# Retention followed by a Mish layer: one copy on another engine, one tile's columns reordered, two PSUM banks exchanged

## The chip, the cores and the metric

The kernel runs on one core of a Trainium2 chip. TensorE (PE) multiplies and writes to PSUM, eight banks of 128 x 512 float32; VectorE (DVE) and ScalarE (ACT) copy and compute out of PSUM; GpSimd (POOL) works between tiles in SBUF and issues most loads; SyncE (SP) issues stores. The metric is the device time of one execution in microseconds, the median of several runs. Beside it one execution was recorded with the profiler; times of single instructions come from that one.

## What is computed

Retention over 8 batches, 8 heads, 576 positions and 64 dimensions, and behind it a layer with Mish on the 4608 rows:

```python
scores = scale * np.matmul(q, k.transpose(0, 1, 3, 2))
Dmat = np.where(rel >= 0, gamma[:, None, None] ** rel[None, :, :], 0.0)     # rel = i - j, one gamma per head
attn = np.matmul(scores * Dmat[None], v)
x = attn.transpose(0, 2, 1, 3).reshape(B * S, H * D)       # 4608 x 512
h = x @ w_in                                               # 4608 x 2048
out = (h * np.tanh(softplus(h))) @ w_out                   # 4608 x 512, float32
```

## The kernel before

The 4608 rows are cut into chunks of 128 rows of one batch, 36 in all (the last 64 rows of two batches share one), and four chunks make a tile of 512 rows; there are nine tiles. Tiles 0 and 1 hold the first chunk of every batch, four batches each. The other chunks follow in pairs. `N0` is 8, the first chunk behind the two first tiles.

A tile goes through three stages. First its `xT` is made: x transposed, bf16, 128 partitions by 4 blocks of 128 features (`KC`) by 512 rows. Then `gT` = Mish(x w_in): for each of 16 blocks of `w_in`, TensorE adds four products into an `hp` bank and ScalarE applies Mish (`g1`, lines 587 and 603). Then g times `w_out`, done with seven half-size block products instead of eight: `unit(t, k)` issues half of product i of tile t (`seven`, line 672), and `taken` moves the result out of its bank or adds it to others. The sums that these products need are made by VectorE from `gT` and `w_out` (`g_sum`, line 663; `w_sum`, line 653).

The first chunks need no past: `f_scores`, `f_out` and `f_v` compute them directly. `f_out(1, b, (act, dve))` makes x of tile 1 for two batches in a double bank `sc`, and copies each batch's half to `xT` (line 262), ScalarE the first and VectorE the second. Tile 1 is then multiplied with `w_in` in two halves, two batches each: `g1_half(i, j)` issues eight products of 256 rows for two blocks of `w_in` (line 612) and one Mish of 512 columns (line 614). `x1[j]` is the view of `xT` for half j.

Each batch also carries a state, k transposed times v summed over chunks. `first_states(t, j)` computes the first states of the four batches of tile t into two banks, `st` and `ops` (line 300), half of the rows with j = 0 and the rest with j = 1; `first_states_copy(t, copies)` copies the banks to SBUF with the two engines that it is given (line 311). For tile 1 that is called within the second half of `g1_half`, before its blocks 6 and 7.

From there on chunks come in pairs in a `visit(n, banks, copies)`: the states of the next pair (`states`, line 448), the outputs of this pair into two banks (`outputs`, line 504, and `outputs_end`, line 520), the scores of the next pair (`step_s`, line 402), then the two banks copied to `xT` by ScalarE (line 532), and the scores masked by VectorE (`step_m`, line 408). Each chunk before its visit is scaled by VectorE (`step_p`, line 359, for q and k; `step_v`, line 366, for v) and its q and k are transposed by TensorE (`step_t`, line 382) and copied by ScalarE (lines 385, 386 and 388). `states` leaves a list of sums that VectorE adds up (line 472) and a cast for ScalarE (lines 479 and 482).

The order on every engine is written out by hand: an engine takes its instructions in the order in which the code issues them, and waits are put in where tiles and banks depend on each other. Between the two first tiles and the steady loop stands a list of steps u = 2 to 23, which runs the products of tile 0 (`unit(0, u - 2)`), then those of tile 1 (`unit(1, u - 16)`), the first two visits (u = 16 and u = 22) and the loads of coming chunks. Loads run through GpSimd's queue (line 342); each waits for the chunk two before it to land and for a free buffer.

PSUM is divided into four pools: `sc` has two double banks, `hp` two banks, `st` and `ops` one bank each. A new tile in a pool waits until the one that had the bank before has been read. In `unit` a table, `beside`, names the products that take another pool than `ops`. For tile 1 the products come in the order 4, 3, 2, 1, 6, 5, 7; 4 takes `hp`, 3 takes `st`, 2 and 1 take `ops`, and 6 and 7 are added to the banks of 3 and 5. The second visit (u = 22) stands between the products i = 2 and i = 1 of that tile. `taken` copies product 2 out of its bank with ScalarE (line 697), and product 1 as well (line 703).

Of the kernel before, what the change touches and what calls it, by code (L numbers as in the profile page):

```python
# [16 lines left out]
def kernel(  # L17
# [18 lines left out]
    nc = tc.nc  # L36
    B, H, S, D = q.shape
    assert (B, H, S, D) == (8, 8, 576, 64)
    P = 128
# [4 lines left out]
    KC = d_model // P  # L44
# [15 lines left out]
    N0 = 2 * NCH  # L60
# [12 lines left out]
    ps_st = ctx.enter_context(tc.tile_pool(name="ps_st", bufs=1, space=PS))  # L73
    ps_h = ctx.enter_context(tc.tile_pool(name="ps_h", bufs=2, space=PS))
    ps_o = ctx.enter_context(tc.tile_pool(name="ps_o", bufs=1, space=PS))
# [4 lines left out]
    w_in_t = wpool.tile([P, KC, d_ff], BF16)  # L80
# [19 lines left out]
    fst = {}  # L100
# [133 lines left out]
    x1 = []  # L234

    def f_out(t, b, copy):
        if b == 0:
            xts[t] = xp.tile([P, KC, NCH * P], BF16, name="xT")
            if t == 1:
                x1.extend(xts[1].rearrange("p c k -> p (c k)")  # L240
                          .rearrange("p (j c k) -> p j c k", j=2, c=KC)[:, j] for j in range(2))
        vb = fst[t]["vb"][b]
        if t == 0:
            pool, name = ((ps_h, "hp"), (ps_h, "hp"), (ps_st, "st"), (ps_o, "ops"))[b]
            ot = pool.tile([P, NP, P], F32, name=name)
        else:
            if b % 2 == 0:
                fst[1]["out"] = ps_sc.tile([P, 2, NP, P], F32, name="sc")
            ot = fst[1]["out"][:, b % 2]
        for p in range(NP):  # L250
            for e in range(2):
                nc.tensor.matmul(ot[ds(64 * e, 64), p, :], lhsT=vb[:, 2 * p + e, :],
                                 rhs=fst[t]["sm", b][:, 2 * p + e, :],
                                 start=(p == 0), stop=True, skip_group_check=True)
        if t == 0:

            n = NP if b < 2 else NP // 2
            for p in range(0, NP, n):
                copy(xts[t][:, ds(p, n), ts(b, P)], ot[:, ds(p, n), :])
        elif b % 2:  # L260
            for e in range(2):
                copy[e](x1[b // 2][:, :, ts(e, P)], fst[1]["out"][:, e])  # L262

    def f_state(t, b, engine=nc.gpsimd):

# [42 lines left out]
    def first_states_copy(t, copies):  # L308
        for i in range(2):
            pair = first.tile([P, 2, NP, 64], F32, name="s0", bufs=4)  # L310
            copies[i](pair, s0_banks[t][i])
            for x in range(2):
                s0[4 * t + 2 * i + x] = pair[:, x]
# [117 lines left out]
    def written(products):  # L431
        sync = mybir.DependencyInfo(mybir.DependencyClass.Sync, mybir.DependencyReason.DATA)
        seen = nc.sync.nop()
        for ins in products:
            tc.add_manual_dep(seen.ins, ins.ins.name, sync, reason="row halves and a bank")
        return seen
# [53 lines left out]
    def run(jobs, *how):  # L490
        while jobs:
            jobs.pop()(*how)
# [4 lines left out]
    def outputs(n, both):  # L497

        for x in range(2):
            vs = live[n + x]["vs"]  # L500
            for h in range(NP):
                for j in range(2):
                    for a in range(2):
                        nc.tensor.matmul(both[j][ds(64 * a, 64), h, x, :], lhsT=vs[ds(64 * j, 64), 2 * h + a, :],
                                         rhs=live[n]["sm"][ds(64 * j, 64), h % 2, x, 2 * (h // 2) + a, :],
                                         start=(x == 0 and h == 0), stop=False, skip_group_check=True)

    def outputs_end(n, both, other, seen=None):

        made = []  # L510
        for x in range(2):
            b, c = chunks[n + x]
            qk = live[n + x]["qk"]
            for g in range(2):
                for e in range(2):
                    j = e ^ other
                    state = st_sb[b, c, j] if c < 4 else st_sb[b + j, 4]
                    for a in range(2):
                        r, p = ds(64 * e, 64), 2 * g + a
                        made.append(nc.tensor.matmul(  # L520
                            both[j][ds(64 * a, 64), 2 * g + e, x, :], lhsT=state[r, p, :],
                            rhs=qk[r, 0, p, ds(64 * j, 64)], start=False, stop=True, skip_group_check=True))
                        if seen is not None and len(made) == 1:
                            behind(made[0], seen)
        return made[-4:]
# [8 lines left out]
    def visit(n, banks, copies, masked=True):  # L534


        units = states(n + 2)
        for unit in units[:1]:
            unit()
        both = [pool.tile([P, NP, 2, 64], F32, name=name) for pool, name in banks]  # L540
        outputs(n, both)
        seen = written(outputs_end(n, both, 0))
        if units:
            step_s(n + 2)
        for unit in units[1:]:
            unit()
        outputs_end(n, both, 1, seen)
        outputs_copy(n, both, copies)
        if units and masked:
            step_m(n + 2)  # L550
# [54 lines left out]
    def g1_half(i, j):  # L605

        if 1 not in gts:
            gts[1] = gp.tile([P, nF, NCH * P], BF16, name="gT")
        hp = ps_h.tile([P, 2, 2 * P], F32, name="hp")
        for a in range(2):  # L610
            for c in range(KC):
                nc.tensor.matmul(hp[:, a], lhsT=w_in_t[:, c, ts(2 * i + a, P)], rhs=x1[j][:, c, :],  # L612
                                 start=(a == 0 and c == 0), stop=(c == KC - 1), skip_group_check=True)
        nc.scalar.activation(gts[1][:, ds(2 * i, 2), ds(2 * P * j, 2 * P)], hp, AX.Mish)  # L614

# [19 lines left out]
    NS = 2  # L635
# [40 lines left out]
    dve, act, pool = nc.vector.tensor_copy, nc.scalar.copy, nc.gpsimd.tensor_copy  # L676
# [78 lines left out]
    def unit(t, k):  # L755

        i, half = ORDER.get(t, (4, 2, 1, 3, 6, 5, 7))[k // 2], k % 2
        if half == 0 and i not in LIKE:
            beside = {5: (ps_st, "st"), 4: (ps_h, "hp"), 3: (ps_h, "hp")} if t == 0 else \
                {4: (ps_h, "hp"), 3: (ps_st, "st")} if t < NS else \  # L760
                {2: (ps_st, "st"), 3: (ps_st, "st")} if t == nT - 2 else {}
            pool, name = beside.get(i, (ps_o, "ops"))
            banks[i] = pool.tile([P, 2, hD], F32, name=name)
        bank = banks[LIKE.get(i, i)]
        seven(t, i, half, bank, add=i in LIKE)
        if half:
            taken(t, i, bank)
# [252 lines left out]
    for i in range(8):  # L1020
        if i == 1:
            ahead(7)
            load(N0 + 3)
            g_sum(0, 2)
            for m in (7, 4):
                w_sum(m)
        elif i == 4:
            first_states(1, 0)
        elif i == 6:
            first_states(1, 1)  # L1030
            first_states_copy(1, (act, dve))
        g1_half(i, 1)

    queued = [4 * NCH]
# [13 lines left out]
    for u in range(2, 24):  # L1048
        j, w = divmod(u, 4)
        for m in {2: (6,), 3: (3, 1)}.get(u, ()):  # L1050
            w_sum(m)
        if u in (5, 7):
            g_sum(0, 1 if u == 5 else 6)
        if u in ps:
            att(N0 + ps[u], "P")
        if u == 11:
            step_m(N0)
        if u in vs:
            att(N0 + vs[u], "V")
        if u in (19, 21):  # L1060
            g_sum(1, 1 if u == 19 else 6)
        for s in {14: (0, 1), 17: (2, 3)}.get(u, ()):
            send(0, s)
        if w == 0 and j > 0:
            if j < 5:
                load(N0 + j + 3)
            else:
                more_loads(N0 + j + PF)
        if u == 10:
            units = states(N0)  # L1070
            units[0]()
            step_s(N0)
            units[1]()
            run(sums)
        elif u == 16:
            visit(N0, ((ps_o, "ops"), (ps_st, "st")), (act, act), masked=False)
            g_sum(1, 2)
            run(sums)
            att(N0 + 5, "P")
            att(N0 + 4, "V")  # L1080
            step_m(N0 + 2)
        elif u == 22:
            visit(N0 + 2, ((ps_h, "hp"), (ps_h, "hp")), (act, act))
        if u in (13, 20):
            run(casts, act)
        if u in ts_:
            att(N0 + ts_[u], "T")
        if u < nF:
            if u == 15:
                att(N0 + 4, "P")  # L1090
            unit(0, u - 2)
            flush()
        else:
            unit(1, u - nF)
# [136 lines left out]
```

## Time and profile before

| what | before |
|---|---|
| median of 3 runs | 291.44 us (291.42 to 293.78) |
| profiled execution, its time | 292.62 us |
| its span | 290.9 us |
| TensorE busy | 276.6 us, 95% |
| VectorE busy | 220.5 us, 76% |
| ScalarE busy | 160.6 us, 55% |
| GpSimd busy | 154.5 us, 53% |
| granted TensorE clock | 0.998 |
| moved by DMA | 45.95 MB |

The span is what the profiler records between the first and the last instruction; the time of the execution has some 1.7 us around it. A share of busy time is a mean over the whole span, in which stages with different limits follow each other. In a row of the timeline stand the start, the time taken, the engine, the line, the operation, the tile written and the tiles read, the shape, and in brackets the idle time of the engine before it with what ended it. A row of waits has who waited, for whom, and then the total, the number of times and the longest.

### The profile page before, as it was taken

What the parts mean: (1) busy time and instruction counts of PE and PEld (TensorE: products, weight loads), DVE (VectorE), ACT (ScalarE), POOL (GpSimd) and SP (SyncE); (2) the same over time, 40 slices, a digit from 0 to 9 for tenths busy, and PEclk for the clock granted to TensorE, in tenths of its full rate; (3) what the DMA queues carried; (4) which work ended last, traced back from release to release, by engine and by line L of the source; (5) the groups of instructions that cost most, each with busy time, mean ns of one, the idle gap of its engine ahead of it and who ended that gap; (6) DMA issues with size and microseconds to landing.
All of it is one profiled execution on the core that took longest, in us unless ns stands there. A gap on an engine that the chain in (4) does not pass through costs nothing.

```text
span 290.9 us, 9142 instructions
## 1 busy us (share of the span) xinstructions
PE 276.6 (95%) x3960; PEld 205.2 (71%) x3988; DVE 220.5 (76%) x312; ACT 160.6 (55%) x284; POOL 154.5 (53%) x183
## 2 busy tenths in 40 slices
PE   8699999996999989999999999999999999999994
PEld 8567688885877656666666666667666766888783
DVE  4873587899999885888389877883989194778783
ACT  5556566633766654645474646465646455476620
POOL 8487696756581986274818473938240000369500
PEclk9999999999999999999999999999999999999999
DMA  7999999789999597959996999599939001200333
GB/s 152 209 204 218 221 198 217 190 183 227 277 215 202 120 192 221 214 147 138 229 186 186 144 239 190 159 137 245 164 101 146 0 5 72 74 1 2 103 92 97
DMA packets 42600, 45.95 MB, mean 158 GB/s; under 512 B 23872, under 2 KB 32320, under 8 KB 42560
## 3 DMA queue, kind: packets, MB, share of 16 engines
q0 software_dynamic: 15312, 30.15, 50.4%
q1 hardware_dynamic: 26656, 14.69, 25.6%
q8 instruction: 31, 0.51, 0.8%
q10 hardware_dynamic: 592, 0.52, 0.6%
q14 instruction: 9, 0.07, 0.1%
HBM read 36.70 MB, written 9.44 MB: 159 GB/s over the span
## 4 chain that ended last, share of the span: by engine, by line
PE 80%; DVE 9%; issue 3%; DMA 3%; POOL 2%; ACT 1%; POOLq 0%; ACTq 0%; DVEq 0%
PE hp L587 29%; PE ops L672 26%; PE hp L612 4%; PE hp L592 3%; DMA gT<-in_v_dram 3%; PE st L672 2%; DVE qks L359 2%; PE hp L672 2%; PE hp L809 2%; PE sc L809 1%; PE sc L448 1%; DVE vs L366 1%; DVE room L663 1%; PE sc L880 1%; PE sc L402 1%
## 5 line engine op out<-in xcount | busy, mean ns | idle before, releaser
L587 PE MATMUL hp<-xT,w_in_t 128*128 128x512 bf16 x380 | 96.9, 379 | 1.4
L603 ACT ACTIVATE gT<-hp 128x512 bf16<-128x512 f32 x113 | 67.1, 598 | 45.8 <-PE hp L587 40.2
L672 PEld LDWEIGHTS <-room 128*128 128x128 bf16 x656 | 63.4, 98 | 14.6 <-DVE room L663 0.6
L587 PEld LDWEIGHTS <-w_in_t 128*128 128x128 bf16 x412 | 39.9, 98 | 35.3 <-issue 0.2
L359 DVE TENSOR_TENSOR qks<-qkraw,gqk 128x512 bf16<-128x512 f32 x56 | 46.9, 886 | 9.4 <-DMA qkraw<-in_k_dram 6.2
L663 DVE TENSOR_TENSOR room<-gT 128x2048 bf16<-128x2048 bf16 x43 | 52.7, 1245 | 1.1 <-ACT gT L603 1.1
L672 PE MATMUL ops<-room,room 128*128 128x256 bf16 x336 | 42.0, 273 | 0.5 <-DVE room L663 0.4
L366 POOL TENSOR_TENSOR vs<-vraw,gv 128x512 bf16<-128x512 f32 x20 | 26.0, 1319 | 22.6 <-ACT gT L603 22.5
L342 POOL DMA_DIRECT2D vraw<-in_v_dram x24 | 21.2, 887 | 25.9 <-issue 24.7
L672 PEld LDWEIGHTS <-gT 128*128 128x128 bf16 x288 | 27.5, 98 | 7.9 <-issue 1.7
L342 POOL DMA_DIRECT2D qkraw<-in_q_dram x24 | 21.6, 899 | 13.6 <-DVE vs L366 3.1
L408 DVE TENSOR_TENSOR sm<-sc,mask 128x1024 bf16<-128x1024 f32 x14 | 17.1, 1218 | 15.5 <-PE sc L402 14.0
L672 PE MATMUL ops<-w_out_t,room 128*128 128x256 bf16 x224 | 27.2, 273 | 0.0
L827 POOL TENSOR_TENSOR vraw<-vraw 128x256 f32<-128x256 f32 x7 | 6.4, 908 | 38.2 <-ACT vraw L821 38.1
L342 POOL DMA_DIRECT2D qkraw<-in_k_dram x24 | 21.3, 886 | 0.0
L612 PE MATMUL hp<-xT,w_in_t 128*128 128x256 bf16 x128 | 15.2, 273 | 0.4 <-DVE xT L262 0.4
L472 DVE TENSOR_TENSOR total<-sc,total 128x256 f32<-128x256 f32 x32 | 13.5, 422 | 2.2 <-PE sc L448 1.4
L672 PE MATMUL ops<-room,gT 128*128 128x256 bf16 x112 | 13.9, 272 | 1.3 <-issue 1.2
L532 ACT CAST xT<-hp 128x512 bf16<-128x512 f32 x18 | 9.7, 588 | 7.5 <-PE hp L520 7.5
L612 PEld LDWEIGHTS <-w_in_t 128*128 128x128 bf16 x128 | 12.1, 98 | 2.2 <-issue 0.7
L592 PE MATMUL hp<-xT,w_in_t 128*128 128x256 bf16 x88 | 13.2, 273 | 0.0
L614 ACT ACTIVATE gT<-hp 128x512 bf16<-128x512 f32 x16 | 9.6, 597 | 6.4 <-PE hp L612 5.4
(188 smaller groups left out, 432.0 us busy)
## 6 DMA issues: line engine op xcount, KB each, us to landing
out_dram<-res SPq DMA_DIRECT2D x29, 256.0 KB, 4.3
qkraw<-in_q_dram POOLq DMA_DIRECT2D x24, 256.0 KB, 5.5
qkraw<-in_k_dram POOLq DMA_DIRECT2D x24, 256.0 KB, 6.2
vraw<-in_v_dram POOLq DMA_DIRECT2D x24, 256.0 KB, 6.1
w_out_t<-in_moe_w_out_dram POOLq DMA_DIRECT2D x4, 512.0 KB, 10.7
w_in_t<-in_moe_w_in_dram POOLq DMA_DIRECT2D x6, 256.0 KB, 8.0
out_dram<-res SPq DMA_DIRECT2D x9, 128.0 KB, 2.4
gT<-in_v_dram POOLq DMA_DIRECT2D x2, 512.0 KB, 8.5
```

The source lines that it names most:

```text
L342: ins = nc.gpsimd.dma_start(out=t, in_=src[b, :, ds(P * c, P), :].rearrange("h p d -> p h d"))
L359: nc.vector.tensor_tensor(slots[:, :, y], heads[:, :, y], factors[:, :, y].unsqueeze(3).to_broadcast([P, NP, 2, D]), op=OP.mult)
L366: ins = engine.tensor_tensor(vs, live[n]["v"], gv[:, c, :].unsqueeze(2).to_broadcast([P, H, D]), op=OP.mult)
L408: nc.vector.tensor_tensor(sm.rearrange("p e x n i -> p (e x n) i"), live[n]["sc"].rearrange("p e x n i -> p (e x n) i"), mask.unsqueeze(1) ...
L472: nc.vector.tensor_tensor(new[:, k], st[:, j, x], total[b], op=OP.add)
L532: copy(xts[t][:, :, ds(P * s, 2 * P)].rearrange("p h (x j i) -> p j h x i", x=2, j=2)[:, j], both[j])
L587: nc.tensor.matmul(to, lhsT=w, rhs=x, start=first, stop=last)
L592: nc.tensor.matmul(to[:, ts(j, n)], lhsT=w, rhs=x[:, ts(j, n)], start=False, stop=False, skip_group_check=True)
L603: done[t] = nc.scalar.activation(gts[t][:, f, :], hp, AX.Mish)
L612: nc.tensor.matmul(hp[:, a], lhsT=w_in_t[:, c, ts(2 * i + a, P)], rhs=x1[j][:, c, :], start=(a == 0 and c == 0), stop=(c == KC - 1), skip_ ...
L663: engine.tensor_tensor(to, g_half(t, *a), g_half(t, *b), op=op_)
L672: nc.tensor.matmul(bank[:, half, :], lhsT=g[:, f, ts(half, P)], rhs=w[:, f, :], start=(f == 0 and half == 0 and not add), stop=(f == hF - ...
```

## The change

Three edits. The second copy of `first_states_copy(1, ...)` goes from VectorE to ScalarE, so that ScalarE makes both. The half view `x1[j]` gets the batch ahead of the feature block: each batch's 4 x 128 columns lie in one run, the copies of line 262 write 512 columns in a row, and the products of line 612 read their 256 rows as two runs of 128. And in the second visit the first of the two outputs takes the bank `ops` instead of one of `hp`, while product i = 1 of tile 1 takes `hp` instead of `ops`. The order of the instructions on TensorE, GpSimd and SyncE stays; VectorE has one copy less and ScalarE one more.

```diff
@@ f_out
-                          .rearrange("p (j c k) -> p j c k", j=2, c=KC)[:, j] for j in range(2))
+                          .rearrange("p (j e c k) -> p j e c k", j=2, e=2, c=KC)[:, j] for j in range(2))
...
-                copy[e](x1[b // 2][:, :, ts(e, P)], fst[1]["out"][:, e])
+                copy[e](x1[b // 2][:, e], fst[1]["out"][:, e])
@@ g1_half
-                nc.tensor.matmul(hp[:, a], lhsT=w_in_t[:, c, ts(2 * i + a, P)], rhs=x1[j][:, c, :],
+                nc.tensor.matmul(hp[:, a].rearrange("p (e k) -> p e k", e=2), lhsT=w_in_t[:, c, ts(2 * i + a, P)], rhs=x1[j][:, :, c, :],
                                  start=(a == 0 and c == 0), stop=(c == KC - 1), skip_group_check=True)
@@ unit
-                {4: (ps_h, "hp"), 3: (ps_st, "st")} if t < NS else \
+                {4: (ps_h, "hp"), 3: (ps_st, "st"), 1: (ps_h, "hp")} if t < NS else \
@@ the second half of tile 1
-            first_states_copy(1, (act, dve))
+            first_states_copy(1, (act, act))
@@ the steps u = 2 to 23
         elif u == 22:
-            visit(N0 + 2, ((ps_h, "hp"), (ps_h, "hp")), (act, act))
+            visit(N0 + 2, ((ps_o, "ops"), (ps_h, "hp")), (act, act))
```

## The prediction

> **What bounds the kernel now.** I read the stages first, because a mean over the span hides that they have different limits. The columns of this view are the stretch, then for TensorE matmul, its weight load, VectorE, ScalarE and GpSimd the busy time and the number of instructions, then the granted clock, the DMA share and GB/s.
>
> ```profile
> 49.50:66.00 16.50, 16.50 (x248) 14.48 (x248) 14.35 (x21) 8.01 (x15) 11.46 (x14) 1.00 0.79 185
> 66.00:80.50 14.50, 11.46 (x347) 9.97 (x346) 14.33 (x25) 8.27 (x14) 9.12 (x12) 1.00 0.98 254
> 80.50:150.00 69.50, 67.82 (x1026) 46.39 (x1037) 54.31 (x74) 39.94 (x70) 42.44 (x46) 1.00 0.93 188
> 150.00:245.00 95.00, 94.32 (x1353) 63.34 (x1365) 73.42 (x92) 53.18 (x93) 37.09 (x40) 1.00 0.73 141
> ```
>
> Of these stretches TensorE is nearly full in all but the one from 66 to 80.5 us; there VectorE is full (14.33 of 14.50). The waits of TensorE, from 49 to 81 us and then from 81 us to the end, say what the holes are worth:
>
> ```profile
> PE sc L382 <- DVE total L472: 1.6, 1, 1.6
> PE ops L504 <- DVE res L747: 0.9, 1, 0.9
> PE ops L672 <- DVE room L663: 0.4, 1, 0.4
> ...
> PE ops L672 <- issue: 1.2, 1, 1.2
> PE ops L672 <- ACT gT L603: 0.2, 1, 0.2
> ```
>
> So three waits of 2.97 us together (1.62, 0.90, 0.45), all behind VectorE, and after 81 us nearly nothing. What VectorE is late with is read from its timeline:
>
> ```profile
> 47.31 2.35 DVE L653 TENSOR_TENSOR room<-w_out_t 128x2048 bf16<-128x2048 bf16 x2
> 51.82 0.69 DVE L311 COPY s<-ops 128x512 f32<-128x512 f32 x1 [2.15 <-PE ops L300]
> 52.42 1.28 DVE L359 TENSOR_TENSOR qks<-qkraw,gqk 128x512 bf16<-128x512 f32 x2
> ...
> 63.52 1.28 DVE L359 TENSOR_TENSOR qks<-qkraw,gqk 128x512 bf16<-128x512 f32 x2
> 64.72 0.68 DVE L366 TENSOR_TENSOR vs<-vraw,gv 128x512 bf16<-128x512 f32 x1
> ...
> 66.37 1.34 DVE L472 TENSOR_TENSOR total<-sc,total 128x256 f32<-128x256 f32 x3
> ...
> 70.56 0.68 DVE L747 TENSOR_TENSOR res<-ops,dmask 128x512 f32<-128x512 f32 x1
> ...
> 79.20 2.35 DVE L663 TENSOR_TENSOR room<-gT 128x2048 bf16<-128x2048 bf16 x2
> ```
>
> From 52.42 to past 81 us VectorE runs without an idle stretch. Ahead of that it stands still for 2.15 us: the first-state copy of line 311 is next in its order, and its products end only at 51.8. The copy is the last thing that holds VectorE back before its full stretch.
>
> **The copy to ScalarE.** VectorE's next instruction, the first of line 359, then comes right behind the two sums of line 653, which end at 47.31 + 2.35 = 49.66. That is 52.42 - 49.66 = 2.76 us earlier, if its loads are there. They are:
>
> ```profile
> 41.76 0.96 POOL L342 DMA_DIRECT2D qkraw<-in_q_dram  x1
> 42.72 0.89 POOL L342 DMA_DIRECT2D qkraw<-in_k_dram  x1
> ...
> qkraw<-in_q_dram POOLq DMA_DIRECT2D x1, 256.0 KB, 4.8
> qkraw<-in_k_dram POOLq DMA_DIRECT2D x1, 256.0 KB, 5.0
> ```
>
> The two land at 41.76 + 4.8 = 46.6 and 42.72 + 5.0 = 47.7. Later loads have to keep up with a VectorE that is 2.76 us ahead. The tightest is the chunk that line 359 takes at 63.52, which it would now want at 60.76, and its v at 64.72 - 2.76 = 61.96:
>
> ```profile
> 54.00 0.88 POOL L342 DMA_DIRECT2D qkraw<-in_q_dram  x1 [1.92 <-DVE qks L359]
> 54.88 0.88 POOL L342 DMA_DIRECT2D qkraw<-in_k_dram  x1
> 55.75 0.88 POOL L342 DMA_DIRECT2D vraw<-in_v_dram  x1
> ...
> qkraw<-in_k_dram POOLq DMA_DIRECT2D x1, 256.0 KB, 5.9
> vraw<-in_v_dram POOLq DMA_DIRECT2D x1, 256.0 KB, 6.0
> ```
>
> Issued as now, k lands at 60.78 and v at 61.75: just in time. But the issue waits for line 359 itself, so with VectorE ahead GpSimd's queue issues it right behind the load before, up to 1.9 us sooner. I take no loss here, and keep one for the range.
>
> What the lead is worth to TensorE, wait by wait. Its wait at 67.77 is for line 472, which ends at 66.37 + 1.34 = 67.71 and then at 64.95, before TensorE gets there (64.24 + 16 products of 0.109 = 65.99): all of it goes.
>
> ```profile
> 64.24 1.91 PE L672 MATMUL ops<-room,room 128*128 128x256 bf16 x16
> 67.77 0.62 PE L382 MATMUL sc<-ident,qks 128*128 128x128 bf16 x8 [1.62 <-DVE total L472]
> ...
> 71.29 0.22 PE L504 MATMUL ops<-sm,vs 64*64 64x64 bf16 x2 [0.90 <-DVE res L747]
> ...
> 78.87 0.44 PE L504 MATMUL hp<-sm,vs 64*64 64x64 bf16 x32
> ...
> 80.47 1.92 PE L672 MATMUL ops<-room,room 128*128 128x256 bf16 x16 [0.45 <-DVE room L663]
> ```
>
> From row to row that is 67.77 - 66.02 = 1.75 us (0.03 left for the start). The wait at 71.29 is for line 747, done at 71.24 - 2.76 = 68.48; TensorE comes there at 71.29 - 1.75 - 0.90 = 68.64, so the 0.90 goes too, and it is 2.65 us ahead. At 80.47 it wants the first of two sums of line 663, and can be ahead by no more than VectorE: without the rest of the change the gain ends at **2.76 us**.
>
> On ScalarE the copy stands between two Mish calls of line 614.
>
> ```profile
> 51.88 0.58 ACT L311 COPY s<-st 128x512 f32<-128x512 f32 x1
> 52.74 0.60 ACT L614 ACTIVATE gT<-hp 128x512 bf16<-128x512 f32 x1 [0.28 <-PE hp L612]
> ```
>
> Its twin there takes 0.58 us, so a second one ends at 51.88 + 2 x 0.58 = 53.04 at the latest and the Mish of 52.74 starts at most 0.3 late. ScalarE is busy for 8.01 of 16.50 us in this stretch, and TensorE waits for none of its results there (the waits above). Cost: nothing; 0.6 us if that idle time were not there.
>
> **x laid out by batches.** The wish would be that the two copies of line 262 (ScalarE for one batch, VectorE for the other) no longer write interleaved columns and so run side by side. But in the program of the changed kernel VectorE's copy still waits for the same count of ScalarE as before. So this row stays:
>
> ```profile
> 34.99 1.03 PE L612 MATMUL hp<-xT,w_in_t 128*128 128x256 bf16 x8 [0.42 <-DVE xT L262]
> ```
>
> Gain 0; 0.4 us if the wait did go. What is new is the operand that the 128 products of line 612 stream: two runs of 128 columns with a jump between them, where it was one run of 256. No product before reads such an operand, so its price is bounded by rows. Below: no gain, since the columns are as many. Above:
>
> ```profile
> L612 PE MATMUL hp<-xT,w_in_t 128*128 128x256 bf16 x128 | 15.2, 273 | 0.4 <-DVE xT L262 0.4
> ...
> 36.02 0.89 PE sc L195 x16
> 36.92 1.75 PE hp L612 x16
> ```
>
> Two products of 128 columns take 2 x 0.89/16 = 111.2 ns, one of 256 takes 1.75/16 = 109.4 ns (the last two rows are from the chain): 1.8 ns each, 0.23 us in all, if the jump costs what a new product costs. If it drained the array, each product would pay once more what lies between its duration and its pitch, 273 - 109 = 164 ns, 21 us in all. The value I take is 0, nearest to the first.
>
> The Trainium skill (SBUF — State Buffer, Door 1: The DMA port swizzle) says that SBUF is read in lines of 16 bytes and that each step to a new line costs something unless a line is hit twice. A run of 128 bf16 is 256 bytes, so by the rule the jump adds at most one such step per product, and the sum stays as it is; no run of before shows a streamed operand with a jump. The skill's TensorE: Matmul & The Clock Gate (Wait — 56ns, not 53.3ns?) gives each matmul a fixed 2.5 ns beside its columns; the trace's 1.8 ns is near it, and by the page the upper case of 128 products would be an estimated 0.32 us.
>
> **The exchange of banks.** In the second visit one of the two outputs moves from an hp bank to the single ops bank, and the product of lines 665 to 672 that held ops (the fourth of that tile, i = 1) takes hp. The order on TensorE stays. New is what the visit waits for: the ops bank holds the product before it until ScalarE's copy of line 697 has taken it.
>
> ```profile
> 75.63 1.01 ACT L388 COPY qkT<-hp 128x1024 bf16<-128x1024 bf16 x1 [0.73 <-PE hp L382]
> ...
> 78.06 1.02 ACT L388 COPY qkT<-sc 128x1024 bf16<-128x1024 bf16 x1
> 78.96 0.61 ACT L697 COPY dmask<-ops 128x512 f32<-128x512 f32 x1
> ```
>
> From 75.63 ScalarE works through five copies without idle time, line 697 last; it ends at 79.57, while the visit's first output (line 504) starts at 78.87. Both follow TensorE's transposes, so both come 2.65 us sooner and the distance stays: the visit waits 79.57 + 0.05 - 78.87 = 0.75 us for its bank. In TensorE's order the scores, states and all later outputs of the visit stand behind it, then the product at 80.47. That product would have come at 80.02 - 2.65 = 77.37; with the stall it comes at 78.12, after VectorE's sum (80.47 - 2.76 = 77.71), whose 0.45 us wait is thereby hidden. So TensorE ends 80.47 - 78.12 = **2.35 us** ahead; the exchange gives back 0.4 of the 2.76. It returns nothing later: the product's copy out of its hp bank, as long as line 697's, ends at 78.12 + 1.75 + 0.61 + 0.1 = 80.58, and TensorE wants that bank only after one more group of eight half products, 8 x 0.109 after 79.87, at 80.74.
>
> After 81 us TensorE is the bound, and the later loads are released by ScalarE's results, so the lead is kept to the end. **Sum:** the profiled execution took 292.62 us with a span of 290.9; less 2.35 it would be 290.27, span 288.55. The median shown is 291.44, 1.18 below the profiled time; the same step gives **289.1 us** (0.8% less). What a measurement can tell from no change is about 1%, 2.9 us, so this counts as within.
>
> **The rivals.**
> (a) The visit does not wait for its bank, because line 697 comes sooner in ScalarE's order than I place it. Then VectorE's sum at 80.47 decides: 291.44 - 2.8 = 288.6 us. For it: ScalarE idles 0.73 us before 75.63. Against: that idle time ends with TensorE's own transposes.
> (b) The lead is eaten by loads. The 5.9 and 6.0 us of the tight chunk have no room; were they 1 us slower and issued as now, VectorE would lead by about 1.8 instead of 2.76, and TensorE by some 1.7 less part of the stall: 290.0 us. For it: a DMA share of 0.98 from 66 to 80.5 us. Against: 0.79 before, and the issue that moves up.
> (c) The layout does nothing at all (my forecast) or frees the copy after all: 0.4 us more at 34.99, 288.7 us. The count in the program speaks against it.
> (d) Slower: the jump in the streamed operand of line 612. From 2.35 us / 128 = 18 ns a product it decides; at 164 ns the time is 291.44 - 2.35 + 21 = 310 us. Against: runs of 128 columns are what the transposes stream, at 55.6 ns each.
>
> **How the numbers follow.** Forecast 0.55, (a) 0.15, (b) 0.17, (c) freed 0.05, (d) 0.04, and 0.04 for a start that is held back for a reason not seen, with no change in time. The range reaches from a little below (a) to beyond (b): 288.3 to 290.8 us. Faster by over 1% (below 288.5) takes nearly half of (a) and (c) and a little of the forecast, 0.15; slower by over 1% is (d) and a mishap, 0.05; the rest, 0.80, is within.
>
> **What would show it.** Right: line 359 starts at about 49.7 on VectorE with no copy before it; the waits of TensorE for lines 472 and 747 are gone; its product after the second visit starts near 78.1; a new wait of about 0.75 us of line 504 behind ScalarE's line 697; products of line 612 still at 1.75 us for 16; VectorE's copy of line 262 still behind ScalarE's. Wrong: line 359 waits for a load before 66 us, TensorE's lead at 81 us is under 1.7 or over 2.9 us, or line 612 slows.

## The result, and the profile after

The changed kernel takes 290.86 us in the median of 22 runs, the kernel before 292.63 in 22 runs beside it. The ratio, of the means, is 0.9929, with a 95% interval from 0.9902 to 0.9955: 0.7% less, some 2.1 us, where 2.35 us were forecast. It leaves out the slow executions, those over 1.5% above the fastest of the same kernel (three of the changed kernel, one of before). A later comparison of the same kernel gave 0.9948 (0.9909 to 0.9986). Both intervals lie below 1, so it is a gain, and a small one.

The profiled execution has a span of 287.4 us against 290.9. Its stages, in the same columns as before:

```profile
49.50:66.00 16.50, 16.50 (x254) 14.64 (x252) 16.40 (x24) 9.04 (x17) 12.05 (x15) 1.00 0.91 208
66.00:80.50 14.50, 13.77 (x363) 11.91 (x362) 14.36 (x23) 8.67 (x17) 9.58 (x13) 1.00 0.93 238
80.50:150.00 69.50, 68.69 (x1030) 46.45 (x1038) 54.28 (x75) 41.45 (x72) 40.87 (x44) 1.00 1.03 189
```

VectorE is now busy for 16.40 of the 16.50 us ahead of 66 (14.35 before), and TensorE for 13.77 instead of 11.46 of the 14.50 behind it. The waits of TensorE, first from 49 to 81 us, then from 79 us to the end:

```profile
PE ops L504 <- ACT dmask L697: 0.7, 1, 0.7
...
PE ops L672 <- issue: 0.2, 1, 0.2
PE ops L672 <- ACT gT L603: 0.2, 1, 0.2
```

The three waits behind VectorE (2.97 us) are gone, and the one that the exchange of banks was to bring is there (the first row). VectorE's timeline shows the cause, with no copy ahead of line 359:

```profile
46.91 2.35 DVE L653 TENSOR_TENSOR room<-w_out_t 128x2048 bf16<-128x2048 bf16 x2
49.18 1.29 DVE L359 TENSOR_TENSOR qks<-qkraw,gqk 128x512 bf16<-128x512 f32 x2
...
60.27 1.29 DVE L359 TENSOR_TENSOR qks<-qkraw,gqk 128x512 bf16<-128x512 f32 x2
...
75.96 2.35 DVE L663 TENSOR_TENSOR room<-gT 128x2048 bf16<-128x2048 bf16 x2
```

On TensorE the marks to compare are the first product of line 612, the two visits' outputs (line 504) and the product i = 1 behind the second visit. On ScalarE it is line 697, which frees the bank:

```profile
34.58 1.03 PE L612 MATMUL hp<-xT,w_in_t 128*128 128x256 bf16 x8 [0.43 <-DVE xT L262]
...
65.58 0.61 PE L382 MATMUL sc<-ident,qks 128*128 128x128 bf16 x8
...
76.50 0.22 PE L504 MATMUL ops<-sm,vs 64*64 64x64 bf16 x2 [0.68 <-ACT dmask L697]
...
77.59 1.92 PE L672 MATMUL hp<-room,room 128*128 128x256 bf16 x16
```

```profile
74.94 1.02 ACT L388 COPY qkT<-sc 128x1024 bf16<-128x1024 bf16 x1
75.84 0.61 ACT L697 COPY dmask<-ops 128x512 f32<-128x512 f32 x1
```

Starts differ from execution to execution (34.99 before, 34.58 here), so I measure from the first product of line 612 to product i = 1, and call that the stretch: 80.47 - 34.99 = 45.48 us before, 77.59 - 34.58 = 43.01 us after. The change made it 2.47 us shorter. The two spans differ by 3.5 us, and the rest does not belong to the change: 0.41 is the earlier start, 0.95 is a wait of TensorE for its own issue near 108 us that was 1.16 and is 0.21, and 0.3 goes the other way, a wait of a weight load (line 587) for its issue at 81.92, just behind the stretch, that the kernel before does not have and the changed kernel's second profiled execution does not either. The waits at "issue" are taken up at the end.

### The profile page after: what moved, and what is told of

It is laid out like the page before. It is cut to its first block, busy times and chain, and to the rows that moved or that the text cites. A ratio compares the mean times of both kernels' runs of the same rounds, so it can differ in the third digit from the quotient of the medians.

```text
span 287.4 us, 9142 instructions
## 1 busy us (share of the span) xinstructions
PE 276.9 (96%) x3960; PEld 205.2 (71%) x3988; DVE 220.2 (77%) x311; ACT 161.0 (56%) x285; POOL 154.1 (54%) x183
## 4 chain that ended last, share of the span: by engine, by line
PE 89%; DMA 3%; ACT 2%; POOL 2%; issue 2%; DVE 1%; POOLq 0%; ACTq 0%; DVEq 0%
PE hp L587 30%; PE ops L672 27%; PE hp L612 5%; PE hp L672 5%; PE st L672 4%; PE hp L592 3%; DMA gT<-in_v_dram 3%; PE hp L809 2%; PE sc L448 2%; PE sc L402 1%; PE sc L809 1%; PE sc L880 1%; POOL gT L112 1%; PE hp L520 1%; PE sc L382 1%
## 5 line engine op out<-in xcount | busy, mean ns | idle before, releaser
L672 PE MATMUL ops<-room,room 128*128 128x256 bf16 x320 | 40.1, 273 | 0.1
```

The lines of the kernel that those rows point to most:

```text
L672: nc.tensor.matmul(bank[:, half, :], lhsT=g[:, f, ts(half, P)], rhs=w[:, f, :], start=(f == 0 and half == 0 and not add), stop=(f == hF - ...
```

## The experiments

All are compared by the stretch in one profiled execution, where 0.1 us counts, and by the ratio to the kernel before, whose interval is 0.3 to 0.8% either way. The granted TensorE clock within the stretch is 1.00 in each of these executions.

| kernel | stretch, us | ratio (95% interval) |
|---|---|---|
| before | 45.48 | 1 |
| the change | 43.01, again 42.90 | 0.9929 (0.9902 to 0.9955) |
| copy alone | 42.65 | 0.9918 (0.9882 to 0.9955) |
| exchange of banks alone | 45.72 | 0.9988 (0.9946 to 1.0029) |
| layout alone | 45.81 | 0.9996 (0.9956 to 1.0036) |
| the change without the exchange | 42.65 | 0.9895 (0.9858 to 0.9932) |
| copy on VectorE, later | 43.68 | 0.9958 (0.9919 to 0.9996) |
| copy, x in two PSUM tiles | 42.48 | 0.9904 (0.9866 to 0.9943) |
| copy, and x copies on ScalarE | 41.95, again 41.94 | 0.9863 (0.9814 to 0.9912), again 0.9893 (0.9852 to 0.9934) |
| these two together | 43.59 | 0.9887 (0.9811 to 0.9964) |
| the change, line 697 first | 43.78, again 42.68 | 0.9911 (0.9873 to 0.9950), again 0.9914 (0.9874 to 0.9953) |

### The three edits one by one

The copy on ScalarE alone:

```diff
-            first_states_copy(1, (act, dve))
+            first_states_copy(1, (act, act))
```

> The first-state copy on ScalarE alone, layout and banks as before. Measure: the time on TensorE from the first product of line 612 to the product i = 1 of tile 1 (the one that stands behind the second visit); it is 45.48 us before (34.99 to 80.47) and 43.01 after (34.58 to 77.59). Theory (VectorE was held by the copy's wait and everything behind it came 2.76 us late): 45.48 - 2.76 = 42.7 us, that is 0.3 less than with all three edits, no wait behind line 697, some 0.3 us of wait behind line 663; time 2.8 us below before. Rival (the exchange of banks is what lets the lead through, because the product i = 1 in the ops bank would now wait for line 697): 43.0 us or more, with a wait of i = 1 behind ScalarE.

The stretch is 42.65 us, and the product i = 1 waits 0.45 us for line 663 and not for ScalarE:

```profile
36.73 1.03 PE L612 MATMUL hp<-xT,w_in_t 128*128 128x256 bf16 x8 [0.42 <-DVE xT L262]
...
79.38 1.92 PE L672 MATMUL ops<-room,room 128*128 128x256 bf16 x16 [0.45 <-DVE room L663]
```

So this line of the diff gives 2.83 us, more than all three edits together, and the rival that the exchange lets the lead through falls.

The exchange alone, with the two edits of the diff that concern banks (in `unit` and at u = 22) and no other:

> The exchange of banks alone. Theory: the visit waits 0.75 us for line 697's copy, the wait of 0.45 for line 663 is hidden in it, the stretch from the first product of line 612 to product i = 1 is 45.48 + 0.3 = 45.8 us, time 0.3 us above before, too little for the runs to tell. Rival (the exchange brings part of the gain): under 45.2 us.

Measured 45.72, 0.24 longer; the waits of TensorE in the stretch are those of before for lines 472 and 747, and a third, new one in place of that for line 663:

```profile
PE ops L504 <- ACT dmask L697: 0.6, 1, 0.6
```

The layout alone, with the edits in `f_out` and `g1_half`:

> The layout by batches alone. Theory: VectorE's copy of line 262 still follows ScalarE's (idle 1.12 and 0.77 before it, as before), TensorE's wait of 0.42 before its first product of line 612 stays, 16 products of line 612 take 1.75 us, the stretch stays 45.48 and the time is that of before. Rival (contiguous writes or a free copy gain, or the jump in the operand costs): the 0.42 goes, or 16 products take over 1.78 us.

The wait of 0.42 stays (0.43), and so does VectorE's place behind ScalarE at line 262. The stretch is 45.81, 0.33 over the forecast, and a late store is the reason rather than the layout. Up to the transposes of the chunk N0 + 4 nothing differs: before they come at 74.99 - 34.99 = 40.00 us of the stretch, here at 74.77 - 34.78 = 39.99. Then ScalarE waits for a store to land:

```profile
77.37 0.58 ACT L710 COPY res<-st 128x512 f32<-128x512 f32 x1 [0.94 <-DMA out_dram<-res]
...
79.95 0.45 PE L402 MATMUL sc<-qkT 64*64 64x64 bf16 x32 [0.66 <-ACT qkT L388]
```

Line 710 writes into a row buffer that earlier stores still read. Here ScalarE waited 0.94 us for the last of them, and line 388 behind it delayed the scores of the visit. The changed kernel has the same layout and waits for no store there, in either of its profiled executions. The operand with the jump costs nothing: the 48 products in a row in tile 1's stage take 5.41 us before and after, and a single one 273 ns in both.

The change without the exchange:

```diff
-                {4: (ps_h, "hp"), 3: (ps_st, "st"), 1: (ps_h, "hp")} if t < NS else \
+                {4: (ps_h, "hp"), 3: (ps_st, "st")} if t < NS else \
...
-            visit(N0 + 2, ((ps_o, "ops"), (ps_h, "hp")), (act, act))
+            visit(N0 + 2, ((ps_h, "hp"), (ps_h, "hp")), (act, act))
```

> The changed kernel without the exchange of banks: copy on ScalarE and layout by batches. Theory: the stretch is 42.7 us as with the copy alone, 0.3 less than with all three edits, and the waits are those of the copy alone. Rival: 43.0 or more, since the exchange is needed.

42.65 us, the very stretch of the copy alone, so the layout costs nothing. The exchange costs the changed kernel 0.36 us against its first profiled execution and 0.25 against its second. The runs do not tell the two kernels apart: their intervals overlap (0.9895 against 0.9929).

### Was it the wait or the work?

The copy stays on VectorE and moves behind the first chunk's scaling. `late` is a list that the copy is put into:

```diff
-            copies[i](pair, s0_banks[t][i])
+            if copies[i] is None:
+                late.append(lambda pair=pair, bank=s0_banks[t][i]: dve(pair, bank))
+            else:
+                copies[i](pair, s0_banks[t][i])
...
-            first_states_copy(1, (act, dve))
+            first_states_copy(1, (act, None))
...
     att(N0, "P")
     att(N0, "V")
+    late.pop()()
```

> The copy stays on VectorE with layout and banks of before, but stands behind the first chunk's scaling (lines 359 and 366 of before) instead of ahead of it. Theory (what cost 2.76 us was 2.15 of waiting and 0.6 of work at the head of VectorE's full stretch): the scaling starts at 49.7, the copy comes at 51.8 with 0.35 of waiting, so the lead is 2.76 - 0.6 - 0.35 = 1.8 us; TensorE loses its wait for line 472, keeps some 0.8 for line 747, and the stretch from the first product of line 612 to product i = 1 is 45.48 - 1.8 = 43.7 us; time 1.8 us below before. Rival (VectorE's load counts, not where the wait stands; the copy has to leave the engine): at most what is before, 45.5 us.

43.68 us, 1.80 less than before, with VectorE as busy as it was (40.50 us in the stretch, 40.37 before). Its copy has line 314 here and waits 0.34 us, where before it waited 2.15:

```profile
49.39 1.29 DVE L364 TENSOR_TENSOR qks<-qkraw,gqk 128x512 bf16<-128x512 f32 x2
50.59 0.69 DVE L371 TENSOR_TENSOR vs<-vraw,gv 128x512 bf16<-128x512 f32 x1
51.62 0.69 DVE L314 COPY s<-ops 128x512 f32<-128x512 f32 x1 [0.34 <-PE ops L300]
```

So the greater part of the gain is the place of a wait in an engine's order. The engine that makes the copy is worth the rest, 43.68 - 42.65 = 1.03 us: 0.6 of work and 0.4 in which VectorE still stands. This split rests on the profiled executions; the intervals of the two ratios overlap (0.9958 against 0.9918).

### What holds VectorE's copy of line 262?

The layout of before, the copy on ScalarE, and x of two batches in two PSUM tiles:

```diff
-                fst[1]["out"] = ps_sc.tile([P, 2, NP, P], F32, name="sc")
-            ot = fst[1]["out"][:, b % 2]
+                fst[1]["out"] = [ps_sc.tile([P, 2, NP, P], F32, name="sc")[:, 0] for _ in range(2)]
+            ot = fst[1]["out"][b % 2]
...
-                copy[e](x1[b // 2][:, :, ts(e, P)], fst[1]["out"][:, e])
+                copy[e](x1[b // 2][:, :, ts(e, P)], fst[1]["out"][e])
```

> The copy on ScalarE, banks and interleaved layout as before; x of tile 1 for two batches in two PSUM tiles of the pool sc instead of one. Theory (VectorE's copy of line 262 waits for ScalarE's because both read one PSUM tile, not because they write interleaved columns): both copies start within 0.1 us of each other, VectorE's idle time before line 262 behind ScalarE is gone, TensorE's wait of 0.42 before its first product of line 612 falls to 0.1 or less. VectorE then starts its full stretch up to 0.7 earlier, but the second pair's second tile has to wait for the k0 copies (line 281), up to 0.4 on TensorE; stretch 42.3 to 43.1 us. Rival (the columns written make the wait): VectorE's copy still starts 0.6 behind ScalarE's.

VectorE no longer waits for ScalarE, and the wait of 0.42 ahead of line 612 is gone. In the changed kernel (first two rows) the copies follow each other, with two tiles (last three) they overlap:

```profile
33.22 0.59 ACT L262 CAST xT<-sc 128x512 bf16<-128x512 f32 x1
33.84 0.69 DVE L262 CAST xT<-sc 128x512 bf16<-128x512 f32 x1 [1.12 <-ACT xT L262]
```

```profile
32.61 0.58 ACT L262 CAST xT<-sc 128x512 bf16<-128x512 f32 x1
32.76 0.69 DVE L262 CAST xT<-sc 128x512 bf16<-128x512 f32 x1 [0.51 <-PE sc L252]
33.53 1.04 PE L612 MATMUL hp<-xT,w_in_t 128*128 128x256 bf16 x8
```

What made the wait was the one PSUM tile that both engines read, not the columns that they write: it goes with interleaved columns, and it stays with columns by batches. That tile spans two banks, one for each copy, so it was not a bank that they shared either. The Trainium skill (PSUM — Partial Sum Buffer, Specifications (TRN2)) says that ScalarE and VectorE reach PSUM in parallel at full rate as long as they do not meet in a bank. The trace agrees: side by side the copies take 0.58 and 0.69 us, and one after the other 0.59 and 0.69. The second pair's second tile waits 0.3 us for line 281, as expected; the stretch is 42.48 us, 0.17 less than with the copy alone, and the 0.42 of wait ahead of it is saved on top.

### More of the same, and its limit

ScalarE makes both x copies of the second pair as well:

```diff
             for b in (2, 3):
-                f_out(1, b, (act, dve))
+                f_out(1, b, (act, act))
```

> The copy on ScalarE, banks and layout of before, and ScalarE makes both copies of line 262 for the second pair of batches too. Theory: VectorE leaves out a wait of 0.77 and a copy of 0.6 at 43.7, so its scaling starts 1.4 earlier than with the first-state copy alone, at about 48.3 where before is at 52.42, as the loads are there (47.7); the last wait of TensorE, 0.45 for line 663, goes as well and the stretch is 45.48 - 2.97 = 42.5 to 42.3 us, with time 0.3 below the copy alone. Rival (ScalarE becomes the bound there): a wait of line 612 behind line 614 of 0.3 us or more, or a load not there at 48.3, stretch 42.7 or more.

> The kernel with both first-state copies and the second pair's x copies on ScalarE again, beside the changed kernel: stretch 41.95 us as in its first run, 1.06 less than the changed kernel, so a ratio to before that is 0.3 to 0.4% lower than that of the changed kernel, if waits at 'issue' and at the start are the same on average. Rival: no difference between the two, because the loads take the lead back.

41.95 and 41.94 us: TensorE waits for nothing in the stretch. In the view of its busy time it is full:

```profile
34.34:76.29 41.95, 41.95 (x817) 36.90 (x816) 39.40 (x54) 26.16 (x46) 31.33 (x36) 1.00 1.01 226
```

This is 0.35 to 0.55 us below what I expected; the waits thus cost more than the profile lists. TensorE's busy time shows where the rest was: it was 42.44 us before and is 41.95 now, for the same products. In a row without a break 16 products of line 672 are followed after 1.75 us (63.83 to 65.58 in the changed kernel), but the same 16 ahead of a wait are listed with 1.91 us (at 64.24 before), and the wait is counted from there. So that stop cost TensorE 0.16 us more than its row says. Taken for all three stops this makes an estimated 0.49 us, as much as the busy times differ, and with the listed 2.97 it leaves 0.07 of the 3.53.

Its ratios, 0.9863 and 0.9893, are the lowest of a kernel that was run twice. In the series in which both ran the changed kernel had 0.9948, and the medians were 288.98 and 290.79 us; the intervals still overlap. By the stretch it is the best version found. Behind the stretch both of its executions have a wait at "issue", 0.88 us in the second and this one in the first:

```profile
82.69 0.27 PE L592 MATMUL hp<-xT,w_in_t 128*128 128x256 bf16 x1 [2.20 <-issue]
```

Of the other kernels only the changed one had a wait there, 0.3 us in one execution. In turn these two have none near 105 us, where most of the others wait. Whether the earlier lead brings it on is not shown, and how much of the gain it takes back in other executions is known only through the ratios.

The changed kernel beside it:

> The changed kernel itself again, beside the other two. Theory: ratio 0.992 to 0.993, stretch 43.0 us.

The stretch was 42.90 and the ratio 0.9948, slightly above what was expected, which its interval (0.9909 to 0.9986) includes. The ratio of the best version beside it is 0.55% lower, where 0.3 to 0.4% were expected.

Both together, with two tiles for the first pair and ScalarE's two copies for the second:

> All that the theory favours together: the first-state copies and the second pair's x copies on ScalarE, the first pair's x in two PSUM tiles, no exchange, interleaved layout. Theory: the waits of TensorE for lines 262, 472, 747 and 663 are all gone, 0.42 + 2.97 = 3.4 us in all; the stretch is 42.3 to 42.5 us with another 0.4 ahead of it; time 3.2 us below before, 1.1%. Rival (another resource, the loads or ScalarE, takes over): a new wait of TensorE of over 0.3 us before the product i = 1.

This went wrong in the way of the rival. VectorE comes to its scaling before its load has landed, and line 711 (710 of before) meets a late store again; lines are one further down here:

```profile
47.71 1.29 DVE L360 TENSOR_TENSOR qks<-qkraw,gqk 128x512 bf16<-128x512 f32 x2 [1.10 <-DMA qkraw<-in_k_dram]
...
73.74 0.58 ACT L711 COPY res<-st 128x512 f32<-128x512 f32 x1 [0.99 <-DMA out_dram<-res]
```

43.59 us in that execution. TensorE waits 0.7 us behind the late store and 0.4 for VectorE. From the first product of line 612 VectorE is no further ahead than in the version before: it would be ready after 13.23 us (47.71 - 1.10 - 33.38), there after 13.15. But the stretch begins 0.96 us earlier here, at 33.38, and the load does not come sooner, so the loads are the next limit. Whether the late store belongs to it is not settled, since it appeared with the layout alone too.

### Why the exchange costs

In the changed kernel line 697 is queued behind line 388 on ScalarE. Here the transposes that line 388 copies come later:

```diff
-        if u in ts_:
+        if u in ts_ and u != 21:
             att(N0 + ts_[u], "T")
...
             unit(1, u - nF)
+        if u == 21:
+            att(N0 + ts_[u], "T")
```

> The changed kernel, with the transposes of the chunk N0 + 5 put behind the product i = 2 instead of between its halves, so that on ScalarE line 697 (which frees the ops bank) stands ahead of that chunk's line 388. Theory (the exchange costs because the bank's copy is queued behind line 388): line 697 ends about 1 us earlier against TensorE and the wait of line 504 for it, 0.68 us in the changed kernel, is gone; the scores of line 402 need that chunk's transposed copy and now wait for it up to 0.4 us, so the stretch from the first product of line 612 to product i = 1 comes from 43.01 to 42.6 to 42.8 us. Rival (the wait is the bank's own latency and stays): line 504 still waits 0.5 us or more and the stretch is 43.0 or more.

The first profiled execution did not decide: 43.78 us, more than the 42.6 to 42.8 expected, with a late load (0.40 us on VectorE) and a late store, and still 0.50 of wait at line 504.

```profile
74.39 0.59 ACT L710 COPY res<-st 128x512 f32<-128x512 f32 x1 [0.76 <-DMA out_dram<-res]
```

> The kernel with line 697 ahead of line 388 again. Its first profiled execution had two late transfers in the stretch: a store that line 710 waits for (0.76 us on ScalarE, ahead of line 697) and a load (0.40 us on VectorE), so its 43.78 us did not decide. Theory: in an execution without a late transfer line 504 does not wait for line 697 and the stretch is 42.6 to 42.8 us. Rival: line 504 waits 0.5 us for line 697 with no late store before it.

The second had neither: 42.68 us, no wait of line 504, and the scores wait instead:

```profile
76.30 0.45 PE L402 MATMUL sc<-qkT 64*64 64x64 bf16 x32 [0.34 <-ACT qkT L388]
```

So the 0.68 us were ScalarE's order and not the bank itself. Put first, the copy moves half of the wait to the next user of ScalarE, and the stretch comes to that of the kernel without the exchange (42.65).

## Why the prediction was right or wrong, point by point

- **The copy's wait as the cause.** Right. The scaling starts at 49.18; against the start of its execution that is 2.83 us earlier (52.42 - 49.18 - 0.41), where 2.76 was worked out: the sum took line 653's end for the next start, and rows of VectorE overlap by 0.08 (46.91 + 2.35 = 49.26 against 49.18). The copy alone gives 2.83 of stretch.
- **The three waits.** Right. Line 382 comes at 65.58 without one, and lines 747 and 663 no longer appear.
- **ScalarE's place for the copy.** Right: the Mish behind its pair starts at 52.42, against the start 0.09 us later than before, and TensorE waits for no Mish there.
- **The tight chunk.** Right that it costs nothing: its loads are issued at 52.09 instead of 54.00 (against the start 1.50 us sooner, where up to 1.9 was said), and line 359 takes them at 60.27 without a wait. The rival (b), in which loads eat the lead, did not hold here, but it exists: VectorE waited for a load for 0.40 us with line 697 first and for 1.10 in the combined kernel; in the best version it waited 0.42, at no cost to TensorE.
- **The layout.** Right on both counts, no gain and no loss. The rival (d) falls: a product that streams two runs takes 273 ns as before, and 48 in a row take 5.41 us as before, so that the lower price of 1.8 ns a product does not show either (it would be 0.09 us). The Trainium skill (SBUF — State Buffer, Door 1: The DMA port swizzle) says that each step to a new line of 16 bytes costs something, and gives no price; the trace shows none for one jump a product. Rival (c), a copy that comes free, needed the tile to be split and not the layout.
- **The exchange.** Right in kind, and the wait was 0.68 us where 0.75 was worked out. That it gives back 0.4 of 2.76 was measured as 0.36 and 0.25 in the two executions.
- **The sum.** 2.35 forecast, 2.47 in the stretch, 2.1 in the runs (1.3 to 2.9 by the interval). The difference of 0.12 in the stretch is 0.07 more of lead and 0.05 less given back, 0.36 instead of 0.41. The runs alone could not have told this sum from one that is off by half a microsecond; the marks in the traces do. The 289.1 us started from the first series' 291.44 us, and 291.44 x 0.9929 = 289.4; the 290.86 us stand beside 292.63.
- **The lead is kept to the end.** Right: from product i = 1 to the last group of products (line 880) it is 204.57 us before and 203.92 after, and the 0.65 between them are the waits at "issue" named above (0.95 less, 0.3 more).
- **What was not foreseen.** "After 81 us TensorE is the bound" left out that executions differ by more than the change is worth, through waits that no edit touches (below). And the listed waits, 2.97 us, were taken for all that the holes are worth; with 41.95 us the stretch went 3.53 below before, since a stop cost more than its row says. That did no harm to this forecast, which VectorE's lead bounds, but it made the expectation for the better version too small.

## What to carry to other kernels

When one engine runs full and a second is late by it, look at the last instruction of the full engine that waited before its full run: here the place of that wait in the order was worth 1.80 of 2.83 us, and the copy may go to another engine or simply later. Before reordering data so that two engines can write side by side, see in the program what they wait for; here it was one shared PSUM tile, and splitting it freed them. When adding up what TensorE's waits are worth, compare starts from row to row; here a stop cost 0.16 us more than its bracket says. A bank that is exchanged is free only when its reader is done, so read the queue of the reader's engine as well.

## What the runs showed of the hardware that I had not expected

Between executions the waits put down to "issue" on TensorE ranged from nothing (in four of fourteen) to 3.3 us at one place, the first product after a group near 105 us; the rows are from the combined kernel and from the one before:

```profile
107.77 0.72 PE L673 MATMUL ops<-room,gT 128*128 128x256 bf16 x4 [3.32 <-issue]
```

```profile
109.11 0.60 PE L672 MATMUL ops<-room,gT 128*128 128x256 bf16 x4 [1.16 <-issue]
```

The first product of line 612 started anywhere from 33.4 to 36.7 us. The three late ones (36.5 to 36.7: the copy alone, the change without the exchange, and the second one with x copies on ScalarE) had a mean granted clock of 0.92 in the first 21 us of the span, and the others, at 33.4 to 35.0, one of 1.00. In the pages, where each digit is the clock of a 40th of the span in tenths, the dip is in the third slice; the first row is from the copy alone, the second from the change:

```profile
PEclk9979999999999999999999999999999999999998
PEclk9999999999999999999999999999999999999998
```

In three of the executions line 710 waited 0.76 to 0.99 us for a store, and in a fourth 0.20. Each of these can be as large as the change, so a stretch between two marks, which leaves out the start and the waits behind it, told more than a time: 43.01 and 42.90 us for the change, 41.95 and 41.94 for the best version. It does not leave out late loads and stores (43.78 and 42.68 with line 697 first). What the issue waits are was not tried.
